# A transformer block on one Trainium2 core: where its loads are issued from, how a late modulation is spread, and a new order on every engine

## The chip, the cores and the metric

The kernel runs on one core of a Trainium2 chip. Five engines work side by side, each through its own instructions strictly in order, and wait for each other on semaphores: PE (TensorE, matmuls), DVE (VectorE), ACT (ScalarE), POOL (GpSimd) and SP (SyncE, which computes nothing and issues transfers). ACT can issue transfers too. The transfers of both queues run on the same 16 DMA engines. The metric is device time in microseconds (us) of one execution; smaller is better. Three executions of the kernel before gave 229.87, 231.78 and 234.63 us, median 231.78.

## The reference, cut to what matters

One adaptive-layernorm block over 2048 positions of width 448: a local, dilated attention and then an MLP, both scaled and shifted by six vectors that are computed from one conditioning vector `c`.

```python
mod = silu(c) @ w_mod                    # six vectors of 448: sa, ca, ga, sb, cb, gb
h = layernorm(x) * (1 + ca) + sa
q, k, v = split(h @ wqkv)                # 16 heads of 28
# each position attends to itself and 7 earlier ones, in steps of 2
o = softmax(q . k over the 8 positions) @ v
x = x + ga * (o @ wo)
h = layernorm(x) * (1 + cb) + sb
h = gelu(layernorm(h) @ w1 + b1)         # width 1792; a second layernorm, as the MLP has its own
x = x + gb * (h @ w2 + b2)
```

All inputs and the output are bf16.

## The kernel before, in words

**Layout.** The attention steps by 2, so even and odd positions never meet. A pair of neighbouring positions is kept in one partition, `s` being 0 or 1, and everything is done for both halves of 1024. `x_all` holds x in eight tiles j of 128 pairs. The contraction over 448 runs as seven blocks `kb` of 64 rows; the two halves `s` lie in partitions 0 to 63 and 64 to 127, so that two matmuls of 64 rows run beside each other. For that, wqkv, wo and w1 are loaded twice, once into each half of the partitions: 12.39 MB are read from HBM in all.

**Stages**, by the names in the plan and their lines:
- `ld`/`ldi` (431 to 475): loads. x (433), the first third of w_mod (436), wq, wk, wv (443), b1 (459), the rest of w_mod (460), wo (463), b2 as a broadcast to 128 partitions (465), w1 in four loads (470), w2 in two (474). `wpad` (453 to 457) copies wq and wk into the padded `wqk`.
- `fill` (522): eight idle matmuls at the start. `silu` (526 to 534): Exp on ACT, three small DVE operations. `mcol` (544): sa and ca as columns, on PE.
- `ln1` (559 to 578): statistics on DVE, the power -1/2 on POOL (566), normalization on DVE (578) or ACT (575, with a small DVE operation 572 before it). Tiles 0 and 1 are transposed on PE (603) and modulated on the way out (611, 613); tiles 2 to 7 are transposed by DMA, issued by SP (618, `dti`), and modulated in place (626, `hmod`).
- `qk` (648) and its evictions (657, 659), in three chunks of 256, 256 and 512 positions; `v` (681), nine windows n of 114 positions; attention per window: `lt` (716), exp on ACT (724), mask on DVE (732), `po` (745), the reciprocal and product (753, 758), `otr` (768) and its eviction (776, 778), which overwrites `hT`.
- `later_mod` (871 to 895): the other four vectors (`mbc`, 879): 16 matmuls whose stationary operand is silu(c) repeated over 128 columns, so that each vector arrives in all 128 partitions of PSUM, followed by four evictions (881 to 884); then wo is multiplied by ga (886) and w2 by gb (889), and b1 is turned into a column on PE (893).
- `wo` (792), the first residual add `x1` (795), `ln2` (two layernorms, 808 and 810 between them), its transposition by DMA (820), `w1` (840) with gelu on ACT (848), in four chunks of two tiles; `w2` (864), the second residual add `fin` (866) and the store `st` (868), per tile.

**What sets the order.** `build_plan` lists some 650 operations with their buffers, dependences and an estimated duration per engine. `Plan.solve` (299 to 396) is a list scheduler over these: at each step it takes, among what is ready on an engine, the operation of the highest priority, which is the longest way to the end plus a tuned weight per kind and tile (`CFG['weight']`, lines 35 to 239). Some operations may go to DVE or ACT (`engs` with two entries); the scheduler chooses, and it chooses the PSUM slot (four, `ps`) and the other buffers. In it a load issued on ACT is on a pretended engine of its own ("AQ"):

```python
def load(q, nbytes, fn, wr, rd=(), kind="ld"):
    a = op(kind + "i", {q: 0.07}, fn, wr=wr, rd=rd, lat=0.0)
```

so that the scheduler counts an issue as 0.07 us and not as part of ACT's row; on the chip ACT issues it, in order with its computations. A transfer also holds one of eight semaphores; the ninth transfer waits until the first has landed, on the engine that issues it, and so on in turn. In the built program SP issues x in four loads (tiles 2 and 3, then 4 to 7, then 0, then 1) and one half of wq, wk and wv. ACT issues the first third of w_mod, c, the other halves of wq, wk and wv, the rest of w_mod, wo, w1, b1, b2, fourteen in all, and behind these its first computation, the Exp of `silu`. The two w2 loads come later in its queue.

Of the kernel before, what the change touches and what calls it, by code (L numbers as in the profile page):

```python
# [28 lines left out]
 'lat': 0.12,  # L29
 'mlp_chunks': [(0, 2), (2, 2), (4, 2), (6, 2)],  # L30
 'nact': ['a01', 'a10', 'a20', 'a21', 'a41', 'a51', 'b00', 'b21', 'b30', 'b41', 'b50', 'b51', 'c01', 'c10', 'c40', 'c41', 'c61', 'c71'],
 'qk_chunks': [(0, 256), (256, 256), (512, 512)],
 'slots': 4,
 'sw': 0.13,
 'table': 1.28,
 'weight': {'b1t': -55.2,
            'cst': 151.7,
            'dti': 72.9,
            'dti:0': 58.3,
            'dti:1': 10.7,  # L40
            'dti:2': -78.3,
            'dti:3': 175.3,
            'dti:4': 75.4,
            'dti:5': 9.1,
            'dti:6': -6.2,
            'dti:7': 175.1,
            'exp': 109.0,
            'exp:0': -226.0,
            'exp:1': -49.3,
            'exp:2': -10.4,  # L50
            'exp:3': 63.6,
            'exp:4': 80.5,
            'exp:5': -70.4,
            'exp:6': 55.1,
            'exp:7': -120.8,
            'exp:8': 18.9,
            'fill': 149.6,
            'fin': -81.7,
            'gelu': 221.2,
            'gelu:0': 165.7,  # L60
            'gelu:1': -39.9,
            'gelu:2': -224.4,
            'gelu:3': 17.8,
            'hmod': 60.0,
            'hmod:1': 16.1,
            'hmod:3': 29.8,
            'hmod:7': 60.9,
            'ld': 175.5,
            'ldi': -4.4,
            'ln1': 34.3,  # L70
            'ln1:0': -94.3,
            'ln1:1': 7.0,
            'ln1:2': -47.3,
            'ln1:3': -121.9,
            'ln1:4': 56.0,
            'ln1:5': -37.3,
            'ln1:6': 36.3,
            'ln1:7': -33.1,
            'ln2': 220.1,
            'ln2:0': -94.4,  # L80
            'ln2:1': 116.0,
            'ln2:2': 217.9,
            'ln2:3': 151.4,
            'ln2:4': -199.4,
            'ln2:5': -48.9,
            'ln2:6': -25.7,
            'ln2:7': -122.3,
            'lt': 199.2,
            'lt:0': 68.1,
            'lt:1': -16.3,  # L90
            'lt:2': 5.9,
            'lt:3': 79.3,
            'lt:4': 8.4,
            'lt:5': 24.4,
            'lt:6': -33.4,
            'lt:7': 12.9,
            'lt:8': 33.1,
            'mask': -11.6,
            'mask:0': 48.2,
            'mask:1': -77.4,  # L100
            'mask:2': -20.9,
            'mask:3': 128.2,
            'mask:4': 0.8,
            'mask:5': 168.2,
            'mask:6': 40.4,
            'mask:7': -57.6,
            'mask:8': -115.1,
            'mbc': 167.8,
            'mbc:0': 46.8,
            'mcev': -12.0,  # L110
            'mcol': 135.3,
            'mod': -99.4,
            'mod:0': 147.1,
            'ms': -326.5,
            'oev': -33.6,
            'oev:0': 29.7,
            'oev:1': -27.1,
            'oev:2': -167.7,
            'oev:3': 180.5,
            'oev:4': 8.4,  # L120
            'oev:5': 244.2,
            'oev:6': -60.9,
            'oev:7': -101.9,
            'oev:8': -19.7,
            'onm': -210.0,
            'onm:0': 73.9,
            'onm:1': 22.6,
            'onm:2': -8.8,
            'onm:3': -28.6,
            'onm:4': 10.5,  # L130
            'onm:5': -105.9,
            'onm:6': 31.7,
            'onm:7': 50.6,
            'onm:8': -128.7,
            'otr': 98.6,
            'otr:0': 39.4,
            'otr:1': -2.5,
            'otr:2': -19.6,
            'otr:3': -63.1,
            'otr:4': 71.1,  # L140
            'otr:5': 165.6,
            'otr:6': 32.9,
            'otr:7': 71.4,
            'otr:8': 75.9,
            'po': 235.0,
            'po:0': -81.4,
            'po:1': -3.4,
            'po:2': 307.6,
            'po:3': 204.0,
            'po:4': -244.7,  # L150
            'po:5': 84.2,
            'po:6': 199.1,
            'po:7': -7.9,
            'po:8': 86.3,
            'qk': 10.4,
            'qk:0': -65.0,
            'qk:1': -137.4,
            'qk:2': 63.2,
            'qkev': 72.7,
            'qkev:0': 7.0,  # L160
            'qkev:1': -20.3,
            'qkev:2': 49.5,
            'rec': 317.5,
            'rec:0': 55.8,
            'rec:1': 28.4,
            'rec:2': 21.3,
            'rec:3': 152.2,
            'rec:4': -392.7,
            'rec:5': -2.8,
            'rec:6': -157.1,  # L170
            'rec:7': 32.2,
            'rec:8': 61.7,
            'silu': 202.1,
            'st': -149.8,
            'v': 63.9,
            'v:0': -96.5,
            'v:1': 98.8,
            'v:2': 119.6,
            'v:3': 24.6,
            'v:4': 63.4,  # L180
            'v:5': 87.6,
            'v:6': 31.6,
            'v:7': -39.0,
            'v:8': -8.0,
            'vev': -107.0,
            'vev:0': -80.0,
            'vev:1': 0.2,
            'vev:2': 20.3,
            'vev:3': 45.8,
            'vev:4': -107.7,  # L190
            'vev:5': -1.6,
            'vev:6': 2.8,
            'vev:7': -46.5,
            'vev:8': -111.5,
            'w1': 116.4,
            'w1:0': -16.1,
            'w1:1': 34.1,
            'w1:2': -283.9,
            'w1:3': -9.5,
            'w2': 115.9,  # L200
            'w2:0': -46.3,
            'w2:1': 137.8,
            'w2:2': 21.7,
            'w2:3': -34.0,
            'w2:4': -14.0,
            'w2:5': 22.1,
            'w2:6': -207.4,
            'w2:7': -15.4,
            'w2s': -224.4,
            'w2s:0': -33.3,  # L210
            'wo': 301.0,
            'wo:1': -26.4,
            'wo:2': 117.9,
            'wo:3': 243.1,
            'wo:4': 30.3,
            'wo:5': 79.1,
            'wo:6': 98.3,
            'wo:7': -112.6,
            'wo:8': 73.5,
            'wpad': -48.4,  # L220
            'x1': -19.1,
            'x1:1': 50.8,
            'x1:2': -11.4,
            'x1:3': 96.8,
            'x1:4': 36.8,
            'x1:5': -253.1,
            'x1:6': 98.8,
            'x1:7': -19.5,
            'x1:8': -19.3,
            'x1p': 241.6,  # L230
            'x1p:0': 66.0,
            'x1p:1': -215.7,
            'x1p:2': 39.9,
            'x1p:3': -41.0,
            'x1p:4': 2.2,
            'x1p:5': 94.5,
            'x1p:6': 151.0,
            'x1p:7': 100.6,
            'ztr': 250.0},
 'window': {'ACT': 30.25, 'AQ': 0.0, 'DVE': 0, 'PE': 0.25, 'POOL': 23.3, 'SP': 0.0}}  # L240
# [7 lines left out]
class Op:  # L248
    __slots__ = ("i", "kind", "engs", "fn", "deps", "nd", "succ", "uses", "mode", "func", "pri", "start", "end", "eng", "lat", "bump", "idx")


class Plan:
# [14 lines left out]
    def op(self, kind, engs, fn, rd=(), wr=(), uses=(), mode=None, func=ANYF, after=(), lat=None, bump=0.0):  # L267
        o = Op()
        o.i, o.kind, o.engs, o.fn, o.mode, o.func = len(self.ops), kind, engs, fn, mode, func
        o.lat = self.cfg["lat"] if lat is None else lat  # L270
# [18 lines left out]
    def _touch(self, o, key, write):  # L289
        name, lo, hi = key if isinstance(key, tuple) else (key, 0, 1)  # L290
        h = self.hist.setdefault(name, [])
# [7 lines left out]
    def solve(self):  # L299
        cfg = self.cfg  # L300
        ops = self.ops
        for o in ops:
            o.nd = len(o.deps)
            for d in o.deps:
                ops[d].succ.append(o)
        wt = cfg["weight"]
        topo, left = [o for o in ops if not o.nd], [o.nd for o in ops]
        for o in topo:
            for x in o.succ:
                left[x.i] -= 1  # L310
                if not left[x.i]:
                    topo.append(x)
# [12 lines left out]
        while ready:  # L325
            best = None
            cand = {}
            for o in ready:
                t0 = est0[o.i]
                need = {}  # L330
                for b in o.uses:
                    if b.slot is None:
                        need[b.pool] = need.get(b.pool, 0) + 1
# [723 lines left out]
```

## Time and profile before

| what | value |
|---|---|
| time, median of three | 231.78 us |
| the profiled execution's own time | 232.59 us |
| its span, from first to last instruction | 230.9 us |
| mean granted PE clock | 0.873 |
| busy: PE, DVE, ACT, POOL | 170.8, 119.7, 107.6, 42.8 us |
| read from HBM, written | 12.39 MB, 1.84 MB |
| first v matmul, first wo, first w1, last matmul's end | 48.7, 93.4, 120.2, 226.7 us |

The page cuts the span into 40 slices and gives a row per engine, each digit the busy share of a slice in tenths. PEclk is the clock that PE was granted, in tenths of full speed. DMA is the busy share of the 16 DMA engines. A timeline line reads: start, length, engine (ACTq and SPq are the queues that issue transfers), source line, operation, tiles, count, and in brackets the idle time before it and what ended it. The profiled execution's time is 1.7 us more than its span.

### The profile page before, as it was taken

The page shows a single profiled execution, that of the slowest core. Times are in us where ns is not written, and L with a number is a line of the kernel's source. Part 1 is how long each engine was busy: PE and PEld are TensorE (multiplying, and loading weights), DVE is VectorE, ACT ScalarE, POOL GpSimd, SP SyncE. Part 2 cuts the span into 40 slices and gives each one's busy share as a digit, 9 for nine tenths or more (in the row PEclk, how much of TensorE's full clock was granted, in tenths as well). Part 3 has the DMA queues.
Part 4 walks back from the last instruction along what each step waited for, and adds up shares of the span by engine and source line. Part 5 has one row for each costly group of instructions (what it writes and reads, how often), then busy time and mean ns, then how long its engine had stood idle before and what let it go on. Part 6 is the DMA issues. An engine that isn't in the chain of part 4 may idle for free. (4 is left out here: it accounts for less than half of the span.)

```text
span 230.9 us, 7200 instructions
## 1 busy us (share of the span) xinstructions
PE 170.8 (74%) x3263; PEld 116.5 (50%) x3263; DVE 119.7 (52%) x278; ACT 107.6 (47%) x145; POOL 42.8 (19%) x57
## 2 busy tenths in 40 slices
PE   5000005259958588899969998999999798999992
PEld 1000005135736366444647965896554596587551
DVE  0000009636968468779875648812998958200031
ACT  0000024414784147456764994789461487087000
POOL 6000004020511200135200305010244052110030
PEclk9755555559999659999997999999999999999999
DMA  6999999961323620000430053000021210410012
GB/s 189 310 234 281 216 206 210 203 161 34 50 43 45 179 44 3 6 0 3 26 59 4 0 43 81 7 3 3 34 44 47 43 41 3 82 42 3 0 40 80
DMA packets 23882, 17.89 MB, mean 77 GB/s; under 512 B 13612, under 2 KB 23404, under 8 KB 23852
## 3 DMA queue, kind: packets, MB, share of 16 engines
q10 hardware_dynamic: 7228, 9.35, 18.3%
q1 hardware_dynamic: 16624, 8.09, 16.8%
q8 instruction: 25, 0.41, 0.8%
q14 instruction: 5, 0.04, 0.1%
HBM read 12.39 MB, written 1.84 MB: 62 GB/s over the span
## 5 line engine op out<-in xcount | busy, mean ns | idle before, releaser
L840 PE MATMUL ps<-yT,w 64*128 64x256 bf16 x784 | 44.6, 271 | 3.8 <-DMA yT<-zb 3.3
L840 PEld LDWEIGHTS <-w 64*128 64x128 bf16 x784 | 41.7, 95 | 6.9 <-issue 5.5
L848 ACT ACTIVATE hmw<-ps,b1c 128x512 bf16<-128x512 f32 x56 | 38.2, 687 | 14.9 <-PE ps L840 8.3
L864 PE MATMUL ps<-w,hmw 128*128 128x448 bf16 x224 | 44.1, 353 | 0.8 <-ACT hmw L848 0.8
L566 POOL TENSOR_TENSOR rs<-tv,neg_half 128x2 f32<-128x2 f32 x24 | 19.2, 802 | 76.2 <-DVE tv L564 76.2
L864 PEld LDWEIGHTS <-hmw 128*128 128x128 bf16 x224 | 21.2, 98 | 20.5 <-issue 1.5
L648 PE MATMUL ps<-hT,wqk 64*128 64x256 bf16 (+1 forms) x336 | 28.6, 329 | 2.8 <-ACT vb L690 2.8
L855 POOL TENSOR_TENSOR x1p<-x_all,gbb 128x896 f32<-128x896 bf16 x8 | 16.0, 2006 | 72.6 <-DVE x_all L866 38.7
L544 PE MATMUL ps<-silu,hmw 112*64 112x1 bf16 x112 | 3.1, 192 | 30.8 <-DVE silu L532 30.8
L648 PEld LDWEIGHTS <-wqk 64*128 64x128 bf16 x336 | 17.8, 102 | 12.5 <-issue 4.2
L866 DVE TENSOR_TENSOR x_all<-ps,x1p 128x896 bf16<-128x896 f32 x8 | 8.7, 1087 | 27.1 <-PE ps L864 25.1
L559 DVE BATCH_NORM_STATS2 st<-x_all 128x6 f32<-128x448 bf16 x32 | 19.3, 603 | 0.1
L544 PEld LDWEIGHTS <-hmw 112*64 112x64 bf16 x112 | 3.2, 156 | 31.4 <-issue 26.2
L530 DVE TENSOR_SCALAR e_c<-e_c 112x4 f32<-112x4 f32 x1 | 0.2, 170 | 33.4 <-ACT e_c L526 33.4
L681 PE MATMUL ps<-wv,hT 64*64 64x448 bf16 x252 | 15.7, 392 | 1.8 <-issue 1.4
L526 ACT ACT_TABLE_LOAD x1 | 1.3, 1283 | 33.0 <-DMA wo<-in_A_wo_dram 33.0
L724 ACT ACTIVATE et<-ps 128x912 bf16<-128x912 f32 x18 | 15.7, 932 | 0.9 <-PE ps L716 0.8
L732 DVE TENSOR_TENSOR et<-et,mask 128x912 bf16<-128x912 bf16 x18 | 11.4, 654 | 8.9 <-ACT et L724 8.9
L657 ACT CAST qT<-ps 128x512 bf16<-128x512 f32 (+1 forms) x12 | 8.7, 728 | 12.2 <-PE ps L648 12.2
L792 PE MATMUL ps<-wo,hT 64*128 64x448 bf16 x112 | 13.2, 376 | 1.4 <-issue 0.9
L681 PEld LDWEIGHTS <-hT 64*64 64x64 bf16 x252 | 8.4, 119 | 7.1 <-issue 4.7
L575 ACT ACTIVATE zb<-x_all,nm,rs 128x448 bf16<-128x448 bf16 x6 | 4.5, 759 | 15.3 <-DVE nm L572 9.8
(78 smaller groups left out, 190.9 us busy)
## 6 DMA issues: line engine op xcount, KB each, us to landing
w<-in_B_w_dram ACTq DMA_DIRECT2D x6, 784.0 KB, 19.9
out_dram<-x_all SPq DMA_DIRECT2D x8, 224.0 KB, 2.1
hmw<-in_w_mod_dram ACTq DMA_DIRECT2D x1, 1568.0 KB, 14.5
x_all<-in_A_x_dram SPq DMA_DIRECT2D x1, 896.0 KB, 9.5
hmw<-in_w_mod_dram ACTq DMA_DIRECT2D x1, 784.0 KB, 8.0
w<-in_A_wqkv_dram ACTq DMA_DIRECT2D x2, 392.0 KB, 10.9
w<-in_A_wqkv_dram SPq DMA_DIRECT2D x2, 392.0 KB, 13.2
wo<-in_A_wo_dram ACTq DMA_DIRECT2D x2, 392.0 KB, 16.0
```

Of the source, the lines that this page charges most:

```text
L559: g.nc.vector.bn_stats(out=g.stats[nm][:, j, s, :], in_=src(g, pairs[j], s))
L566: op(kind, {"POOL": 0.6}, lambda g: g.nc.gpsimd.tensor_tensor(out=g.rs[nm][:], in0=g.tv[nm][:], in1=g.neg_half[:, 0:n], op=ALU.pow), rd=[" ...
L648: g.nc.tensor.matmul(o[:, s, 0:n], lhsT=g.wqk[r0:r0 + 64, kb, m, :], rhs=g.hT[r0:r0 + 64, kb, c0(t0):c0(t0 + n)], start=(kb == 0), stop=(k ...
L657: g.nc.scalar.copy(out=dst, in_=g.ps[pq.slot][:, :, 0:n])
L681: g.nc.tensor.matmul(o[64 * half:64 * half + 64, s, 0:D], lhsT=g.hT[r0:r0 + 64, kb, ka:ka + 64], rhs=g.wv[r0:r0 + 64, kb, :], start=(kb == ...
L724: g.nc.scalar.activation(out=g.ebufs[et.slot][:, 912 * hf:912 * hf + 912].rearrange("p (r c) -> p r c", r=2), in_=g.ps[lt.slot][:, :, 0:8 ...
L732: g.nc.vector.tensor_tensor(out=v, in0=v, in1=g.mask[:].rearrange("p a b -> p (a b)"), op=ALU.mult)
L792: g.nc.tensor.matmul(o[:, s, 0:D], lhsT=g.hT[r0:r0 + 64, kb, c0(128 * j):c0(128 * j + 128)], rhs=g.wo[r0:r0 + 64, kb, :], start=(kb == 0), ...
L840: g.nc.tensor.matmul(o[:, s, 0:n], lhsT=g.w1[r0:r0 + 64, kb, ft * 128:(ft + 1) * 128], rhs=g.yTb[yT.slot][r0:r0 + 64, kb, 0:n], start=(kb ...
L848: g.nc.scalar.activation(out=g.hmv(hm.slot)[:, ft, :, 0:n], in_=g.ps[p1.slot][:, :, 0:n], func=ACTF.Gelu_apprx_tanh, bias=g.b1c[:, ft:ft + 1])
L855: op("x1p", {"POOL": 2.1}, lambda g, j=j, xp=xp: g.nc.gpsimd.tensor_tensor(out=g.x1pb[xp.slot][:], in0=g.x_all[:, j], in1=g.gbb2[:].unsque ...
L864: g.nc.tensor.matmul(o[:, s, 0:D], lhsT=g.hmv(hm.slot)[:, ft, s, cc:cc + 128], rhs=g.w2[:, ft, :], start=(ft == 0), stop=(ft == FT - 1))
```

## The change

1. **Loads.** All loads go to SP, except c, the second halves of wq and wk and the first third of w_mod, which stay on ACT. They are cut smaller: x into tiles 0, 1, 2-3, 4-5 and 6-7, the rest of w_mod into two, w1 into eight pieces of 448 columns, w2 into four. In the built program SP issues: x1, x0, wq, wk (one half each), x2-3, x4-5, wv, wo, wo, wv, b2, the transposes of tiles 3 and 2, x6-7, b1, w_mod's last third, w1, w_mod's middle third, w1, the transposes of 7, 4 and 6, w1, w1, the transpose of 5, w1, the broadcasts of g2, sb and gb, w1, that of ga, w1, w2, w1, w2, w2, w2, and then the transposes of the MLP's input and the stores. ACT issues c, wq, wk, then loads its table and computes Exp, and issues the first third of w_mod behind that.
2. **Later modulation.** The four vectors are computed as four column tiles of 32, beside each other, into one row each (partitions 0, 32, 64, 96). One ACT operation evicts the rows, with a bias that adds 1 to g2's. Four DMAs on SP spread each row over 128 partitions. The first window of `wo` on PE comes after ga has been spread and multiplied into wo on DVE, as before.
3. **Order.** `Plan.solve` and its weights are gone. `Plan.place` reads a fixed order of all operations with their engines and buffers, written out in ORDER and SLOTS; the estimated durations in the plan are others. In the built order, PE runs v0, v1, qk of the first chunk, b1's transposition between, qk of the second chunk with lt, po and v2, v3 between, the modulation rows, and only then wo of tile 0; v4 to v7, po2 to po4 and qk of the third chunk follow, and then the first w1; v8 and the last step of attention 4 come after that.
4. **Small.** Sixteen idle matmuls instead of eight; an Exp on a dummy value ahead of all else on ACT; of the eight `wpad` copies, four are on POOL, three on ACT and one on DVE, where three were on ACT and five on DVE; the small operation before a normalization on ACT is done for both halves at once, and for all tiles; the last tile's add and store are done in two halves.

```diff
-    def load(q, nbytes, fn, wr, rd=(), kind="ld"):
-        a = op(kind + "i", {q: 0.07}, fn, wr=wr, rd=rd, lat=0.0)
...
+    def load(q, nbytes, fn, wr, rd=(), bulk=False):
...
+        a = op("ldi", {q: 0.6}, fn, wr=wr, rd=rd, lat=0.0, after=after, bump=0.0 if bulk else pri)
...
+    load("ACT", 900, lambda g: g.nc.scalar.dma_start(out=g.c_col[:], in_=g.c.rearrange("o (p kt) -> p (o kt)", kt=KM)), ["c_col"])
+    load_m("ACT", 0, 2, "wmA")
     load_x(0, 1)
...
+    for pc in range(4):
         for hf in range(2):
             def f(g, pc=pc, hf=hf):
+                a, b = pc * 448, pc * 448 + 448
+                g.nc.sync.dma_start(out=g.w1[64 * hf:64 * hf + 64, :, a:b], in_=g.B_w1[:, a:b].rearrange("(kb p) n -> p kb n", p=64))
+            load("SP", 401e3, f, [("w1", 2 * pc + hf, 2 * pc + hf + 1)], bulk=True)
...
     def later_mod():
-        mb = [P.buf("ps", "mb0"), P.buf("ps", "mb1")]
...
+        mb = P.buf("ps", "mrow")
+        def f_mm(g):
+            for kt in range(KM):
+                for i in range(4):
+                    g.nc.tensor.matmul(g.ps[mb.slot][32 * i:32 * i + 32, 0, 0:D], lhsT=g.silu_bc[:, kt, :], rhs=g.wmod[:, kt, (2 + i) * D:(3 + i) * D],
+                                       start=(kt == 0), stop=(kt == KM - 1), tile_position=(0, 32 * i))
+        op("mod", {"ACT": 0.65}, lambda g: g.nc.scalar.activation(out=g.mrow[:], in_=g.ps[mb.slot][:, 0, 0:D], func=ACTF.Identity, bias=g.one2[:, 0:1]),
+        for i, (nm, dst) in enumerate((("ga", "ga"), ("sb", "sb"), ("g2", "g2"), ("gb", "gb"))):
+            op("mbc", {"SP": 0.6}, lambda g, i=i, dst=dst: g.nc.sync.dma_start(out=getattr(g, dst)[:], in_=g.mrow[32 * i:32 * i + 1, :].unsqueeze(1).to_broadcast([1, 128, D])),
...
-    order = P.solve()
+    order = list(P.place(ORDER.split(), list(map(int, SLOTS.split()))))
```

More of the change, by code (lines that the diff above doesn't have):

```diff
@@ L375, in solve @@
-            o.eng, o.start, o.end = e, t, t + dur
-            free[e] = o.end
-            if e == "PE":
-                mode = o.mode
-            if e == "ACT" and o.func:
-                table = o.func
-            ready.remove(o)
-            order.append(o)
-            for b in o.uses:
-                b.left -= 1
-                if b.left == 0:
-                    last = max([o.end + cfg["lat"]] + [getattr(b, "busy", 0.0)])
-                    slots[b.pool].append((last, b.slot))
-                else:
-                    b.busy = max(getattr(b, "busy", 0.0), o.end + cfg["lat"])
@@ L753, in f_rc @@
             g.nc.vector.reciprocal(out=g.rden[rd_.slot][:], in_=o[:, :, :, DH])
-        b = op("rec", {"DVE": 0.42}, f_rc, uses=[po, rd_], after=[a])
+        b = op("rec", {"DVE": 0.35}, f_rc, uses=[po, rd_], after=[a])
         def f_on(g):
```

577 lines of the change are left out of this document (172 added, 405 removed), and 3 rows, old and new, of the table SLOTS.

## The prediction

> **What bounds the kernel now.** I read the page's slices first, then the timeline of the first 50 us, then stage windows, then the chain that ended last.
>
> ```profile
> PE   5000005259958588899969998999999798999992
> DVE  0000009636968468779875648812998958200031
> PEclk9755555559999659999997999999999999999999
> DMA  6999999961323620000430053000021210410012
> ```
>
> Slices are 5.8 us. For eight of them (to 48 us) the transfers are full and PE nearly idle; DVE wakes in the seventh. Why so late, the timeline tells:
>
> ```profile
> 16.38 13.18 ACTq L470 DMA_DIRECT2D w<-in_B_w_dram  x4
> 29.60 2.50 ACTq L459 DMA_DIRECT2D b1r<-in_B_b_dram  x1
> 32.13 0.86 ACTq L465 DMA_DIRECT2D b_bc<-in_B_b_dram  x1
> 33.03 1.28 ACT L526 ACT_TABLE_LOAD   x1 [33.03 <-DMA wo<-in_A_wo_dram]
> 34.32 0.20 ACT L526 ACTIVATE e_c<-c_col 112x4 f32<-112x4 bf16 x1
> 34.56 0.17 DVE L530 TENSOR_SCALAR e_c<-e_c 112x4 f32<-112x4 f32 x1 [33.36 <-ACT e_c L526]
> ```
>
> ACT issues 14 loads ahead of its first computation. Each reuses the semaphore of the load eight earlier and waits for it, so four w1 loads hold ACT for 13.18 us. DVE's first operation after two memsets needs ACT's Exp, so all layernorms stand behind it (33.36 us idle). PE then waits once more, for the tiny b1r load, behind w1 in the queue: useful PE work starts at 48.67 us. The stages:
>
> ```profile
> 48.50:93.40 44.90, 36.62 (x979) 26.02 (x980) 31.46 (x74) 23.95 (x36) 7.59 (x7) 0.84 0.28 61
> 93.40:120.20 26.80, 23.50 (x457) 12.01 (x450) 22.32 (x49) 15.93 (x18) 7.66 (x6) 1.00 0.17 20
> 120.20:226.75 106.55, 102.68 (x1702) 72.81 (x1702) 55.27 (x122) 60.91 (x83) 20.93 (x18) 0.98 0.14 30
> ```
>
> Columns: stretch, length, busy us of PE, PEld, DVE, ACT, POOL, PE's granted clock, DMA share, GB/s. 93.4 is the first output projection (wo), 120.2 the first w1 matmul. The last stage has 3.9 us of PE idle: little is left there. The chain that ended last agrees, with PE lines 840 and 864 at its head. So the case is the head, to wo.
>
> **Part 1: when PE starts.** Afterwards ACT issues four loads only, Exp stands before the last, and DVE begins with x. The binding load becomes wv: the first PE group is v, and SP issues wv's second half after wo's halves. Ahead of it or with it: six x tiles 1.38 MB, wq, wk, wv, wo 3.21 MB, the first w_mod third 0.80 MB. Rates by windows of before: 307 GB/s over 4 to 12 us (x and w_mod, 112 or 128 partitions), 204 over 12 to 16 and 185 over 26 to 32 (64-partition loads of 896-byte rows). 3.21/0.204 + 2.18/0.307 = 22.8 us, plus 2.1 before data flow and 1 to land: v at **26 us**, 22.7 sooner. mcol, transposes and modulation of the first 256 positions fit before (at 35.2 to 45.1, ten us, in before; from w_mod's landing near 13 they end by 23).
>
> The w1 loads become half as large. [...]
>
> **Part 2: from v to wo on PE.** In row durations: v 4 x 1.52, qk 16 x 0.79 (4.76 for six), lt 8 x 0.37, po 2 x 0.64, otr 2 x 0.41. The modulation: four groups took 3.39 us one after another; as four column tiles between a quarter of it and all of it, I take 0.87, by v's rate (28 matmuls of four tiles, 1.52). Sum 24.8 us. PE starts cold: the clock was 0.50 until 52.6, 4 us after work began, costing 2 us. Before, the stage left 8.3 us idle; bounds 0 and 8.3, I take 5. PE could do wo at 26 + 24.8 + 2 + 5 = **57.8**.
>
> **Part 3: when wo may start.** wo must first be scaled by ga, now a DMA from a row in SBUF to 128 partitions, on SP, after the row's eviction by ACT and six of eight w1 pieces. Behind SP's wait for that row stand the rest of w1 and w2 and all yT transposes; behind DVE's wait for ga stand the masks of attention 2 and 3, the last modulation tile and the first layernorm 2. Ahead of ga: 64-partition loads 5.62 MB, between 27.5 us (204) and 30.4 (185), I take 29; others 4.36 MB/0.307 = 14.2; six hT transposes at 1.4 (two filled 2.8 us of the transfers at 56 to 60) = 8.4; four broadcasts, never seen: 112 KB at the 344 GB/s of 48 to 49 us, where b2's broadcast landed, is 0.33 each, a transpose's rate makes 1.4, and b2's whole way from issue to landing, 16.6, is the far end. I take 0.6 each, nearest b2's bytes. 2.1 + 29 + 14.2 + 8.4 + 2.5 + 2 to land = **58**; scaling (1.79, line 886) makes wo 60, two us behind PE. So both chains meet near 60; before, wo stood at 93.4. Transfers now share these 58 us with PE work that before came after them.
>
> **Part 4: from wo to w1.** PE: wo 3 x 1.5, po 3 x 0.64, v 4 x 1.52, qk2 8 x 1.54 (7.72 for five), otr 2 x 0.41, lt 2 x 0.37 = 26.4, to 86. DVE from 58: scale of wo 1.79, of w2 2 x 1.75, four masks at 0.65, two x1 at 1.09, two onm with rec at 1.3, eight statistics pairs at 0.78, four h passes at 0.64, small ones 2.2: 23.5; two POOL round trips 1.5, the transpose 2.9 from issue: 86. I take 87, that is 27 after wo; before it was 26.8. w2 lands 1.6 MB after ga, 8 us: about when DVE asks.
>
> **Part 5: the rest.** w1 to the last matmul: 106.55, plus v8 (1.52) and otr4 (0.4), which now come later: 108.5, to 195.5. The new order can gain at most the 3.9 idle, or lose as much at ACT, whose in-order queue has layernorm pieces between gelus; I take nothing. Tail: 226.75 to 230.9 was 4.15; the last add and store in halves save half of 1.09 and 0.2: 3.5, span 199.
>
> Costed at nothing: the doubled fill (8 x 0.36, before mcol; uncovered 3 us); the early table load (1.28, while loads land); four weight copies on POOL (nearest row, its 128x912 copy, 1.03; they end before qk, else 1 us each); one eviction instead of four (ACT 1.1, not on the path); the merged nm operations; b1r, now behind the last x (near 31 us, PE at it 32).
>
> **The sum.** The profiled execution took 232.59 us, its span 230.9. 199 + 1.7 = 200.7; that execution stood 0.8 above the median of 231.78, so **200 us**, own range 193 to 208 (ga 55 to 63 by the bounds on rates and broadcasts, last stage plus or minus 3.9).
>
> **Rivals.**
> - Fast loads (0.15): everything flows at 307 GB/s, as two queues' halves together might. ga lands at 2.1 + 32.5 + 8.4 + 1.3 + 2 = 46, v starts at 21, PE reaches wo at 48, twelve sooner: **188**. Against: 26 to 46 us held 185 to 205.
> - Cold PE (0.22): PE is fed in drips, and its clock stays low from v to wo. For: 75 to 90 us of before, with PE 60 to 80% busy after gaps of 1.4 and 2.8 us, got 0.68, 0.50, 0.80. At their mean 0.66, 24.8 becomes 37.6, wo comes at 69, and the end is **209**; at 0.50, 221. Against: DVE has all x early, so fewer gaps. [...]
> - SP takes ACT's place (0.08): SP stops at transposes 3, 7, 5 and at the modulation rows for data that its own later loads delay, and the queue runs dry. At 6 us for each of the four, 24 later: **224**. Then the move does not do what it says. For: SP's waits before a transpose reached 28.9 us. Against: up to eight loads, some 3 MB or 14 us, stand in front.
> - Slower (0.05): the four broadcasts run one by one out of single partitions, and DVE and PE stand at wo meanwhile. From 9.9 us each, 37 in all, the time passes 237; at b2's 16.6 it is **264**. Against: b2's way was mostly queue.
>
> **Chances.** Forecast 0.50, the others as above. A measurement tells from no change about 2%, 227 to 236. Faster 0.91, same 0.04 (the upper part of the SP case), slower 0.05. The range 186 to 220 holds the forecast, the fast case but its lower tail and most of the cold one.
>
> **What would show it.** Right: first v near 26, ga landing near 58, wo near 60, w1 near 87, then about 108 us. Wrong: DVE waiting for ga well past 60 (broadcast or SP), a clock below 0.8 between 30 and 60 (cold), holes in the DMA row before 55 (SP), or more than 6 us of PE idle after the first w1 (the new order).

## The result, and the profile after

The changed kernel took 208.50 us (median of four, 204.44 to 211.99), the kernel before 232.88 beside it (229.87 to 234.63): a ratio of 0.889, 95% interval 0.868 to 0.911. The ratio is taken over the faster executions, 204.44 and 206.00 against 229.87 and 231.78; the changed kernel's other two took 211.00 and 211.99. The profiled execution took 204.44 us, its span 202.4, at a mean granted clock of 0.916 (0.873 before). The forecast was 200, its range 186 to 220.

| us, profiled executions | before | forecast | after |
|---|---|---|---|
| first v matmul | 48.7 | 26 | 26.19 |
| PE could do wo | – | 57.8 | 64.08 |
| ga landed | – | 58 | 65.06 |
| first wo | 93.4 | 60 | 66.91 |
| first w1 | 120.2 | 87 | 95.90 |
| last matmul's end | 226.7 | 195.5 | 199.0 |
| execution | 232.59 | 200.7 | 204.44 |

The page's slices of after, 5.06 us each: PE, DVE, the granted clock, the transfers' busy share and what they moved.

```profile
PE   7206289759476698999999999999979999999993
DVE  3407759735542787997836875598675797100213
PEclk9855569996957699999999999999999999999999
DMA  6999989999989940007002004000221003210101
GB/s 159 247 269 229 208 215 225 197 170 163 138 117 117 237 150 3 0 3 94 3 3 50 3 11 133 3 0 3 49 49 49 0 3 91 45 50 3 45 23 70
```

DVE works from the first slice and PE from the sixth (before: seventh and ninth). But PE has holes from the eighth to the fourteenth slice (35 to 71 us), the clock falls to 0.5 to 0.7 in four of them, and from the ninth on the transfers are still 80% busy or more while the bytes fall to 117 GB/s. The forecast had none of the three. By stage (columns as in the prediction):

```profile
26.20:66.90 40.70, 30.07 (x793) 21.68 (x793) 21.95 (x56) 21.75 (x31) 7.00 (x9) 0.84 1.06 174
66.90:95.90 29.00, 27.12 (x578) 13.60 (x579) 23.95 (x50) 17.81 (x22) 8.73 (x6) 0.95 0.38 75
95.90:199.00 103.10, 101.62 (x1762) 70.07 (x1758) 58.45 (x129) 62.19 (x84) 21.04 (x18) 1.00 0.12 30
```

The first stage lost: 10.6 us idle and 30.07 busy, where 7 (5 and the wait for ga) and 26.8 were reckoned. The last gained: 1.5 us of idle at full clock, where before had 3.9 at 0.98. From the first w1 on, ten of the eleven kernels profiled with this order of PE took between 108.2 and 109.2 us to the end of the execution, so the case is decided ahead of w1. Where the first stage stopped, PE's timeline of after tells:

```profile
38.25 0.28 PE L484 MATMUL ps<-qT,kT 28*64 28x57 bf16 x11
39.55 0.62 PE L484 MATMUL ps<-qT,kT 28*64 28x57 bf16 x53 [1.03 <-issue]
...
42.28 0.93 PE L416 MATMUL ps<-hT,wqk 64*128 64x256 bf16 x13
45.48 1.44 PE L416 MATMUL ps<-hT,wqk 64*128 64x256 bf16 x15 [2.27 <-issue]
...
49.72 0.61 PE L513 MATMUL ps<-vb,et 64*64 64x29 bf16 x53
51.67 0.27 PE L513 MATMUL ps<-vb,et 64*64 64x29 bf16 x11 [1.34 <-issue]
...
53.65 0.39 PE L536 MATMUL ps<-ident,on 57*64 57x57 bf16 x25
57.05 0.26 PE L536 MATMUL ps<-ident,on 57*64 57x57 bf16 x3 [3.01 <-issue]
...
66.91 2.79 PE L560 MATMUL ps<-wo,hT 64*128 64x448 bf16 x14 [2.83 <-DVE wo L664]
```

PE stops in the middle of a run of like matmuls, after 11 of 64, 13 of 28, 53 of 64, 25 of 28, and waits for nothing that the profile shows ("issue"). Count the matmuls between two stops: 53 lt, 14 qk, 16 of the modulation, 32 lt and 13 qk make 128; 15 qk, 32 lt, 28 v, 53 po: 128; 11, 28, 64, 25: 128. (The next two, seen in runs below: 3, 42 qk, 28, 55 lt; and 73 lt, 14 wo, 41 po.) With a weight load each (the page counts 3271 of either) that is 256 instructions. The profile has a queue named "instruction", 25 packets of 16 KB over the execution, one for each 256 or so of PE's 6542 instructions; one begins at 36.7, 43.1, 48.8 and 54.6, each ahead of the end of one of the four stops. So I read the stops as PE waiting for its own program; a table behind the experiments shows how closely the two go together. The kernel before has such stops too, without a stream: 1.40 us at 67.7, with the transfers at 1 GB/s, and 0.86 at 94.1, 640 matmuls further on.

I call these places A (38.5), B (43.2), C (50.3), D (54.0), E (inside the next lt, 73 matmuls from its end), F (po, 41 of 64) and G (otr, two from its end, near 91). PE's order is the same in every kernel below that starts from the changed one, so the places stay at the same instructions.

### The profile page after: what moved, and what is told of

It is laid out like the page before. It is cut to its first block, busy times and chain, and to the rows that moved or that the text cites. A ratio compares the mean times of both kernels' runs of the same rounds, so it can differ in the third digit from the quotient of the medians.

```text
span 202.4 us, 7245 instructions
## 1 busy us (share of the span) xinstructions
PE 168.7 (83%) x3271; PEld 111.9 (55%) x3271; DVE 117.3 (58%) x275; ACT 109.5 (54%) x149; POOL 44.5 (22%) x63
## 3 DMA queue, kind: packets, MB, share of 16 engines
q10 hardware_dynamic: 1520, 1.61, 3.4%
## 4 chain that ended last, share of the span: by engine, by line
PE 65%; DMA 20%; ACT 4%; SPq 4%; issue 3%; DVE 2%; ACTq 1%
PE ps L610 21%; PE ps L634 17%; PE ps L416 11%; DMA wv<-in_A_wqkv_dram 8%; PE ps L560 6%; PE ps L449 6%; DMA w<-in_A_wqkv_dram 4%; DMA ga<-mrow 4%; DMA yT<-zb 4%; SPq L221 2%; SPq L661 2%; PE ps L513 2%; ACT et L492 2%; PE ps L484 1%; ACT zb L343 1%
## 5 line engine op out<-in xcount | busy, mean ns | idle before, releaser
L618 ACT ACTIVATE hmw<-ps,b1c 128x512 bf16<-128x512 f32 x56 | 37.7, 687 | 13.6 <-PE ps L610 10.6
L610 PEld LDWEIGHTS <-w 64*128 64x128 bf16 x784 | 38.5, 94 | 5.9 <-issue 0.7
L330 POOL TENSOR_TENSOR rs<-tv,neg_half 128x2 f32<-128x2 f32 x24 | 20.4, 851 | 78.0 <-DVE tv L328 77.6
L625 POOL TENSOR_TENSOR x1p<-x_all,gbb 128x896 f32<-128x896 bf16 x8 | 15.2, 1894 | 44.8 <-issue 29.9
L416 PEld LDWEIGHTS <-wqk 64*128 64x128 bf16 x336 | 17.1, 101 | 11.6 <-issue 2.9
L643 DVE TENSOR_TENSOR x_all<-ps,x1p 128x896 bf16<-128x896 f32 x7 | 7.6, 1090 | 20.3 <-PE ps L634 20.2
L458 ACT CAST vb<-ps 128x896 bf16<-128x896 f32 x8 | 7.2, 910 | 15.2 <-PE ps L449 15.2
L343 ACT ACTIVATE zb<-x_all,nm,rs 128x448 bf16<-128x448 bf16 x9 | 6.3, 753 | 14.0 <-DVE nm L333 14.0
L563 DVE TENSOR_TENSOR x_all<-ps,x_all 128x896 bf16<-128x896 f32 x8 | 8.7, 1084 | 8.4 <-PE ps L560 8.4
L343 ACT ACTIVATE zb<-h,nm,rs 128x448 bf16<-128x448 bf16 x12 | 8.7, 753 | 7.6 <-DVE nm L333 5.1
L526 DVE TENSOR_TENSOR on<-ps,rden 128x896 bf16<-128x896 f32 x9 | 9.8, 1085 | 2.9 <-PE ps L536 2.7
```

What stands on the lines that cost most here:

```text
L330: op(kind, {"POOL": 0.8}, lambda g: g.nc.gpsimd.tensor_tensor(out=g.rs[nm][:], in0=g.tv[nm][:], in1=g.neg_half[:, 0:n], op=ALU.pow), rd=[" ...
L343: g.nc.scalar.activation(out=dst(g), in_=src(g), func=ACTF.Identity, scale=g.rs[nm][:, idx:idx + 1], bias=g.nm[nm][:, idx:idx + 1])
L416: g.nc.tensor.matmul(o[:, s, 0:n], lhsT=g.wqk[r0:r0 + 64, kb, m, :], rhs=g.hT[r0:r0 + 64, kb, c0(t0):c0(t0 + n)], start=(kb == 0), stop=(k ...
L610: g.nc.tensor.matmul(o[:, s, 0:n], lhsT=g.w1[r0:r0 + 64, kb, ft * 128:(ft + 1) * 128], rhs=g.yTb[yT.slot][r0:r0 + 64, kb, 0:n], start=(kb ...
L618: g.nc.scalar.activation(out=g.hmv(hm.slot)[:, ft, :, 0:n], in_=g.ps[p1.slot][:, :, 0:n], func=ACTF.Gelu_apprx_tanh, bias=g.b1c[:, ft:ft + 1])
L625: op("x1p", {"POOL": 2.05}, lambda g, j=j, xp=xp: g.nc.gpsimd.tensor_tensor(out=g.x1pb[xp.slot][:], in0=g.x_all[:, j], in1=g.gbb2[:].unsqu ...
```

## The experiments

**First and second: the queue alone.** Kernel before, with ten of ACT's loads and both w2 loads issued by SP; then also b1's small load first.

```diff
-g.nc.scalar.dma_start(out=g.b1r[:], ...        # likewise wv, w_mod's rest, wo, b2, w1, w2
+g.nc.sync.dma_start(out=g.b1r[:], ...
```
```diff
     order = P.solve()
+    b1 = next(o for o in order if o.i == 30)
+    order.remove(b1)
+    order.insert(1, b1)
```

> The kernel before, its scheduler untouched, with ten of the loads that ACT issued ahead of Exp (half of wv, the rest of w_mod, wo, w1, b1, b2) and the two w2 loads issued by SP at the same places of the order. Theory A, the whole head was ACT's queue: Exp runs near 4 us instead of 34, layernorm starts when x lands near 12, v starts near 26 and the end comes about 20 us sooner, 212. Theory B, there were two locks on the head: PE stands at b1's transposition, whose load is still behind w1 in the queue and lands near 47, so v starts near 47, only 2 us sooner; but the layernorms of tiles 2 to 7 are done by then and the first modulated second chunk is ready sooner (70.5 in before, near 62 now): about 225.

> As the run before it, and b1's load moved to the second place of the order. Theory A: no further gain, 212 in both. Theory B: this takes the second lock away, v starts near 24, but SP now issues all loads before the first transposition of the second chunk, which lands behind w1 near 48; the second chunk of qk starts near 50 instead of 70.5 and the end comes about 18 us sooner than before: 214. Left over to the changed kernel would then be its order and its spread rows, some 6 us.

Measured: 229.04 us, ratio 0.989 (0.983 to 0.995), and 218.23 us, 0.948 (0.940 to 0.957). PE's timeline of the first:

```profile
18.88 1.67 PE L603 MATMUL ps<-ident,zb 128*128 128x128 bf16 x14 [4.42 <-ACT zb L575]
50.69 0.19 PE L893 MATMUL ps<-ident,b1r 14*128 14x14 bf16 x1 [30.14 <-DMA b1r<-in_B_b_dram]
```

and of the second:

```profile
30.12 5.44 PE L681 MATMUL ps<-wv,hT 64*64 64x448 bf16 x56 [9.14 <-DMA wv<-in_A_wqkv_dram]
...
55.21 1.36 PE L716 MATMUL ps<-qT,kT 28*64 28x57 bf16 x96 [10.00 <-ACT kT L657]
```

With the issuing queue alone DVE's first layernorm starts at 12.62 and not at 35.05, and PE's transposes at 18.88 and not at 40.13. But PE then waits 30 us for 3.5 KB of b1 (6.75 in the kernel before), and v begins at 50.81, 2 us later than before: two locks in a row, and opening one gives 1%, less than either theory asked. With both open, 5% (214 us was asked); then wv sets v's start, at 30.12, and PE's ten us pass while ACT and DVE wait (8.86 and 9.51 us) for the transposes of h, which SP issues from 37.55 on, behind w1 and the first of w2. The other half of the gain belongs to the rest of the change: the order of loads and of work, the spread rows and the small edits. No run here takes these apart.

**Third: ga first.** The changed kernel with the spread of ga ahead of the others.

```diff
 # ORDER, SP's words (188 ga, 190 g2, 189 sb, 191 gb; 38 to 52 w1; 63 to 69 w2)
-40S 46S 146S 44S 190S 189S 191S 50S 188S 48S
+40S 46S 146S 188S 44S 190S 189S 191S 50S 48S
```

> The changed kernel with one line of the order moved: ga is spread first, before g2, sb, gb and one w1 piece. If ga's landing (65.1) alone holds wo, ga lands near 56 and wo starts near 58, 8 us sooner, and the end comes 6 to 8 us sooner. If PE reaches wo at 64.1 by its own chain, as the trace shows it, wo starts at 64 to 65 and the gain is 2 to 3 us at most.

Measured: 210.11 us, 0.909 (0.904 to 0.914); profiled 209.15. The time is no better than the changed kernel's. ga landed at 56.3, nine us sooner, and wo began at 66.71, no sooner than in after (66.91), waiting for attention's exponentials and not for ga. The stops had grown: 0.74, 2.00, 1.61, 4.65 at A to D, 3.88 at F. The wait for ga was no lock of its own; PE was as late by its stops.

**Fourth: bulk loads late.** The spreads as in the third, and all w2 and w1 loads behind them.

```diff
-26S 34S 28S 38S 24S 42S 162S 138S 154S 40S 46S 146S 44S 190S 189S 191S 50S 188S 48S 63S 52S 65S 67S 69S
+26S 34S 28S 24S 162S 138S 154S 146S 188S 190S 189S 191S 63S 65S 67S 69S 38S 40S 42S 44S 46S 48S 50S 52S
```

> The changed kernel with all w1 and w2 loads issued behind the spread rows, ga first; the PE order is the same. Theory F: the PE gaps inside runs of matmuls that wait for nothing (1.0 at 38.5, 2.3 at 43.2, 1.3 at 50.3, 3.0 at 54.0) are the fetch of PE's next instructions, slowed by the loads; with the loads gone from 27 to 50 us each of the four falls to 1.4 or less (the 1.4 of before, where the transfers were quiet), the clock stays up, transposes land in 3 to 4 us instead of 5 to 6, and wo starts near 57: the end 6 to 9 us sooner, unless w2 or w1 then lands too late (w2 near 58, w1 near 76, asked for at 75 and 96 in the changed kernel). Theory G: the gaps are waits on other engines; they keep their lengths, and wo gains only what an earlier ga gives, 2 to 3 us.

Measured: 199.65 us, 0.856 (0.848 to 0.863), its interval below that of the changed kernel (0.868 to 0.911). A, B and C were gone and D had 1.12. wo began at 61.39, 5.5 us sooner than in after (57 was asked): 1.9 of it comes from shorter stops, 2.5 from the wait for ga and 2.1 from qk behind D at full clock, and a wait of 1.2 for a mask takes from that. But E and F opened:

```profile
54.67 0.62 PE L490 MATMUL ps<-qT,kT 28*64 28x57 bf16 x55 [0.33 <-ACT kT L431]
59.96 1.07 PE L490 MATMUL ps<-qT,kT 28*64 28x57 bf16 x73 [4.66 <-issue]
```

The loads were issued from 54.97 on, and F (64.9 to 66.15) stands under them, at 308 GB/s. E doesn't. While it lasted, the transfers were 80% busy and moved little:

```profile
55.30:59.90 4.60, 0.00 (x0) 0.00 (x0) 0.91 (x1) 0.05 (x1) 0.00 (x0) 0.90 0.80 57
```

That is the mark of the four spreads, as the runs without w1 show below; the last was issued at 50.98 and landed 10.2 us later. So a stop goes with whatever the transfers do at it and just ahead of it, loads or spreads.

**Fifth: wv's second half ahead of wo**, on top of the fourth.

```diff
-20S 30S 32S 18S
+20S 18S 30S 32S
```

> The kernel of the fourth experiment (all w2 and w1 loads behind the four spread rows, ga first; 199.65 us) with one issue moved more: wv's second half goes out ahead of wo's two halves instead of behind them. In the fourth experiment PE waits 4.45 us for it, until v at 26.3. Theory H (the head's last loads set everything up to wo): v starts near 22, when the transposed tiles are ready, and wo, the first w1 matmul and the end all come 4 us earlier: wo at 57.5, time 195.5. Rival (other chains, tiles 2 to 7 and the modulation rows, gate what follows v): v starts at 22 but second-chunk qk stays near 51.4 and wo near 61, time 199 to 200.

Measured: 199.06 us (195.95 to 206.06), 0.859 (0.848 to 0.871): no difference from the fourth that the runs show. In the profiled execution, 195.95 and the shortest of all kernels, v began at 24.47, held by ACT's last piece of hT and no more by wv, wo at 58.48, w1 at 87.72; E still had 4.39. The move is worth two us at v; the spread between executions is wider.

**Two bulk loads in flight**, on top of the fourth: each late load overlaps the one two places before it.

```diff
-                a, b = pc * 448, pc * 448 + 448
+                a, b = pc * 448 - (8 if pc else 0), pc * 448 + 448
...
-    for (a, b) in ((0, 4), (4, 7), (7, 11), (11, 14)):
+    for (a, b) in ((0, 4), (7, 11), (3, 7), (10, 14)):
```

> The kernel of the fourth experiment (199.65 us), but each of the twelve late w2 and w1 loads reads a strip that the load two places earlier wrote (the same values), so that it waits for that one to land: two bulk loads in flight instead of up to eight, 0.3 MB more bytes in all. In the fourth experiment PE has a gap of 4.66 us at 55.2 within a run of lt matmuls that waits for nothing, with a packet of PE's instructions inside it and eight loads queued. Theory Q (PE's instruction fetch waits behind the bytes that the loads have queued): the gap shrinks below 2 us, wo comes near 58, time 197. Rival S (any full stream of transfers slows the fetch, however deep the queue): a gap of 4 to 5 us stays and the time with it, 199 to 200. The loads take until 84 at worst, ahead of w1 at 92, so they cost nothing else.

Measured: 203.11 us, 0.883 (0.874 to 0.892). E fell to 2.04, as the theory of the queue's depth asks, but F had 1.54 and G, which the loads reach now (177 GB/s over 76 to 90), 1.27; and PE stood 3.02 us for a mask at 46.5, before any late load was issued (1.21 in the fourth). E stands under the spreads here too (43 GB/s over 51 to 58), which the edit leaves alone, and PE came to it 2.3 us later than in the fourth. So the run settles nothing on the depth, and it is slower.

**What the spreads do.** Two variants of the changed kernel: the spreads from 128 partitions instead of one; and w1 left out but for one seventh (so not the reference's MLP).

```diff
-in_=g.mrow[32 * i:32 * i + 1, :].unsqueeze(1).to_broadcast([1, 128, D])
+in_=g.b2_bc[:]
```
```diff
-g.nc.sync.dma_start(out=g.w1[64 * hf:64 * hf + 64, :, a:b], in_=g.B_w1[:, a:b].rearrange("(kb p) n -> p kb n", p=64))
+g.nc.sync.dma_start(out=g.w1[64 * hf:64 * hf + 64, 0, a:b], in_=g.B_w1[0:64, a:b])
```

> The changed kernel, with the four spreading transfers reading the 128x448 tile of b2 (128 partitions) instead of one row in one partition each; bytes, order and waits stay, and the later modulation's values are left out of the result. In the changed kernel they took 6.7 to 8.5 us from issue to landing, and ga came at 65.06, 8.3 after its issue at 56.8. Theory R (a single partition as the source of 128 descriptors is what makes them slow and holds the transfers at 107 to 133 GB/s): they land in 3 to 4 us, ga near 61, wo by PE's 64, time 3 us less, near 205.5 by the slower or 201.5 by the faster of the changed kernel's runs. Rival (they stand in the queue behind the w1 loads like everything else): 6 to 8 us again, wo at 66 to 67, no gain.

> The changed kernel, with six sevenths of every w1 load left out (each of the eight issues fetches 64 rows of 896 bytes; the rest of w1 is zeros from one memset on DVE while it waits for x), so the MLP's result is not the reference's; PE's program is the same. Theory F (PE's gaps inside runs of matmuls, 1.03 us at 38.5, 2.27 at 43.2, 1.34 at 50.3, 3.01 at 54.0, 0.83 at 70.2, are its instruction fetch held up by the bulk loads): those up to 57 shrink to 0.5 us or nothing, the granted clock over 46 to 62 is above 0.85, PE is ready for wo by 57, ga lands near 56, the time is 198 to 200; the gap at 70 stays with the w2 loads. Rival (the fetch, or the program's own order, makes these gaps whatever the loads): gaps of 1 to 3 us at the same instructions, wo not before 62.

Measured, one execution each: 204.89 and 202.86 us. The times say little beside the changed kernel's 204.44 to 211.99; the traces say more. With the wide source two spreads landed in 5.3 and 4.6 us (6.7 to 8.5 in after), the transfers moved 257 GB/s over 56 to 66 (122 in after), and DVE scaled wo at 64.69 without waiting for ga; but D grew to 5.09 and the end stayed. Without w1, A, B and C shrank to 0.61, 0.63 and 0.42, as theory F said; D, against it, grew to 4.65. The transfers of that run from 49 to 53 us:

```profile
DMA  9199922599550995228995509952299949599742
GB/s 54 9 36 54 36 9 9 18 54 36 18 18 0 54 54 18 9 9 27 45 36 18 18 0 54 54 18 9 9 45 45 81 72 236 36 54 72 63 36 45
DMA packets 168, 0.16 MB, mean 39 GB/s; under 512 B 11, under 2 KB 167, under 8 KB 167
## 3 DMA queue, kind: packets, MB, share of 16 engines
q1 hardware_dynamic: 167, 0.14, 81.3%
q8 instruction: 1, 0.02, 1.4%
```

The engines are 81% busy at 39 GB/s: 0.813 x 16 x 4 us over 167 packets is 0.31 us for each, where the late loads of the fourth experiment took 0.065 (108.7% of 16 engines over 9 us, 2426 packets). The copies that all read one SBUF partition held the engines here without moving much, and a packet of the instruction queue lies among them (52.36 to 53.24).

**Both gone.** The last two edits together.

> The run without w1's loads (one seventh of each is left, the rest of w1 is zeros), and also the four spreading transfers reading a 128x448 tile from 128 partitions instead of one row in one partition each, so the later modulation's values are left out too. In the run without w1's loads the early gaps within PE's matmuls shrank (1.03 to 0.61, 2.27 to 0.63, 1.34 to 0.42 us), but one of 4.65 us stood at 50.2, three instructions before the end of an otr group, while the spreads alone kept the transfers 81% busy at 39 GB/s. Theory G (a spread from one partition occupies the DMA engines and holds up PE's instruction fetch just as bulk loads do): with both gone the gap is below 1 us, the transfers are nearly idle over 50 to 56, the spreads land in 2 to 3 us, PE is ready for wo by 57 to 58, and the time is 197 to 199. Rival (the gap belongs to PE's own stream of short instructions): 3 to 5 us at the same otr group, time 201 to 203.

Measured, one execution: 196.53 us.

```profile
53.38 0.22 PE L537 MATMUL ps<-ident,on 57*64 57x57 bf16 x3 [1.45 <-issue]
...
62.76 0.37 PE L514 MATMUL ps<-vb,et 64*64 64x29 bf16 x23 [1.22 <-issue]
```

These are D and F, the only stops left before w1 of more than 0.3 us; I had asked for less than 1 at D. D: 4.65 with the spreads from one partition, 1.45 without, all else alike. The clock was 1.00 from 36 to 90 us, wo began at 58.62 and w1 at 88.02, 7.9 us sooner than in after. So the stops go with both kinds of transfer: with the bulk loads at A, B and C, and at D with either alone (4.65 with the spreads, 5.09 with the loads and a wide source).

**Issued by ACT.** The changed kernel with wo, b1, b2, w1 and w2 issued by ACT at the same places of the order.

```diff
-g.nc.sync.dma_start(out=g.w1[...                # likewise wo, b1, b2, w2
+g.nc.scalar.dma_start(out=g.w1[...
```

> The changed kernel, with wo, b1, b2, w1 and w2 (sixteen loads) issued by ACT, each at the same place of the written order, instead of SP; everything else stays. Theory B (the issuing queue matters because a reused semaphore holds the issuing engine): ACT, whose evictions and layernorm pieces stand between those loads, waits for a load eight transfers back several times, 2 to 8 us each, PE's matmuls wait for ACT's evictions, first v is past 28, wo past 72, the time 212 to 225. Rival (only the order of the loads matters): v at 26 to 27, wo at 66 to 68, time 204 to 210.

Measured, one execution: 207.64 us, within what the rival gave; wo began at 70.60, between the two theories. v began at 25.43 and ACT was not held up by loads; one late transposition kept DVE idle for 8.07 us, PE then 6.99 for a mask. A to D don't stop in this run: ACT reaches its w1 loads at other times, the transfers moved 96 GB/s over 34 to 42 us (183 in after), and C's packet came while PE waited for the mask. With this order the issuing engine matters little for the time. What held ACT in the kernel before was fourteen loads placed ahead of its first computation.

**Two tries for a better kernel.** On top of the fifth, the rows go to HBM and are spread from there; and then also all w2 and w1 loads behind the first residual sum.

```diff
+                if i == 0:
+                    g.nc.sync.dma_start(out=g.rows[:], in_=g.mrow[0:128:32, :])
+                g.nc.sync.dma_start(out=getattr(g, dst)[:], in_=g.rows[i:i + 1, :].to_broadcast([128, D]))
...
+    g.rows = drp.tile([4, D], BF16, name="rows")        # drp: a pool in DRAM
```
```diff
+            if a == 0:
+                g.nc.sync.dma_start(out=g.gate[:], in_=g.x_all[0:1, 0, 0, 0:64])
# ORDER: the twelve loads moved behind 271D, the first residual sum
```

> The kernel of the fifth experiment (bulk loads behind the spreads, wv's second half ahead of wo; 199.06 us, its faster runs 195.95 to 199.39), with the four rows written once to HBM (3.5 KB) and spread by four loads from there, instead of from one SBUF partition each. There ga landed 6.4 us after its issue at 44.77, and a gap of 4.39 us stood at 52.7 in PE's lt matmuls, spreads and w2's first loads flowing. Theory G (the spreads at 38 to 45 GB/s hold up the fetch): the write takes 2 us, the four spreads land within 3 to 4 us more (112 KB each at 300 GB/s is 0.4), ga at 50, gap below 1.5 us, wo 3 us earlier, median 196. Rival S (any stream holds up the fetch, and w2's loads now flow through the same place): the gap stays at 4 to 5 us, time 199.

> The kernel of the run with the rows in HBM (200.44 us; wo at 60.2), with a store of 128 bytes of the first residual sum ahead of the twelve w2 and w1 loads in SP's queue, and these moved behind that sum in the order, so that no load starts before about 64 us. There, gaps of 1.80 us at 57 (lt) and 4.66 us at 63.4 (po) stood in PE while w2 and w1 ran at 258 GB/s. Theory F (bulk transfers hold up the fetch): with no transfer but transposes and spreads before 64 the first gap falls below 1 us and the second below 1.5, wo comes at 58 to 59, the clock stays at 1.00 from 50 to 66, and w1 at 90; the loads (4.8 MB at 205 to 230 GB/s) end at 87, before w1 needs them, and PE's matmuls of that stretch are long ones (v, qk of 512), which use few instructions per us: median 194 to 196. Rival 1 (the gaps only move to where the loads go): gaps of 3 to 5 us in all over 66 to 88, median 199 to 201. Rival 2 (w2 or w1 land too late): DVE waits for w2 at 72, PE for w1 past 90, median over 201.

Measured: 200.44 us, 0.870 (0.865 to 0.875), and 201.25 us, 0.870 (0.863 to 0.877); profiled 204.18 and 203.11. From HBM the last three spreads landed in 3.5 to 4.4 us (6.4 to 10.1 in the fifth), and over 50 to 51.5 us, where they flow alone, a packet took 0.053 us (23.6% of 16 engines, 106 packets) and not 0.31. But w2 and w1 then began 51.7 us into the run, and the stops were E 1.80 and F 4.66. With the gate:

```profile
56.00:66.00 10.00, 8.21 (x304) 5.58 (x298) 8.62 (x14) 6.75 (x9) 2.24 (x2) 1.00 0.04 10
66.00:76.00 10.00, 8.64 (x106) 4.13 (x104) 7.43 (x16) 6.26 (x8) 4.14 (x4) 1.00 1.05 261
76.00:90.00 14.00, 8.93 (x254) 5.24 (x252) 8.23 (x21) 8.12 (x11) 1.87 (x3) 0.98 1.19 187
```

Over 56 to 66 the transfers are idle, and neither E nor F stops; wo began at 60.13. Over 76 to 90, with 187 GB/s, G stops, and w1 began at 94.74:

```profile
83.92 0.38 PE L546 MATMUL ps<-ident,on 57*64 57x57 bf16 x26
89.07 0.21 PE L546 MATMUL ps<-ident,on 57*64 57x57 bf16 x2 [4.77 <-issue]
```

That is the first rival of its expectation: the gap only moves. I had taken the stretch for one of long matmuls, and it has two windows of v and one of attention in it. The stops in us, by run and place (a dash: none over 0.3; the fifth has 0.62 and the run with two in flight 0.49 at two further multiples of 128):

| run | A | B | C | D | E | F | G |
|---|---|---|---|---|---|---|---|
| after | 1.03 | 2.27 | 1.34 | 3.01 | – | 0.83 | – |
| ga first | 0.74 | 2.00 | 1.61 | 4.65 | – | 3.88 | – |
| bulk late (fourth) | – | – | – | 1.12 | 4.66 | 1.27 | – |
| wv first (fifth) | – | – | – | 1.23 | 4.39 | 0.40 | – |
| two in flight | – | – | – | – | 2.04 | 1.54 | 1.27 |
| wide source | 1.18 | 1.45 | 1.36 | 5.09 | 1.14 | – | – |
| bulk on ACT | – | – | – | – | 1.24 | – | – |
| no w1 | 0.61 | 0.63 | 0.42 | 4.65 | – | 0.83 | – |
| no w1, wide source | – | – | – | 1.45 | – | 1.22 | – |
| rows in HBM | – | – | – | – | 1.80 | 4.66 | – |
| loads after the sum | – | – | – | – | – | – | 4.77 |

Where the time of a stop passes, the packets of 16 KB tell. In the table: when PE began the first matmul behind the multiple of 128 before, when the packet for the next 256 instructions began and ended in the transfers, and when PE went on behind the multiple that it belongs to.

| run, place | multiple before | packet | PE goes on | stop |
|---|---|---|---|---|
| no w1, wide source, D | 49.56 | 50.42 to 51.73 | 53.38 | 1.45 |
| no w1, D | 47.81 | 52.36 to 53.24 | 54.83 | 4.65 |
| loads after the sum, E | 54.43 | 56.36 to 57.29 | 58.77 | – |
| bulk late (fourth), E | 51.29 | 57.50 to 58.42 | 59.96 | 4.66 |
| no w1, wide source, G | 79.65 | 80.70 to 82.00 | 83.32 | – |
| loads after the sum, G | 80.65 | 86.32 to 87.70 | 89.07 | 4.77 |

At all 35 stops of the table before, PE went on 1.2 to 1.7 us after the end of a packet, and the packet itself took 0.9 to 1.5. What differs is its start: in the table, 0.9 to 1.9 us after the multiple before where PE stops briefly or not at all, 4.5 to 6.2 where it stops for over 4.6. So the length of a stop goes with the packet's start, and not with the packet's own time.

The best kernels are the fourth and the fifth, 3 to 4% below the changed one by their ratios to before. They don't remove the stops either: in sum 8.48 us in after, 7.05 and 6.64 in these two.

## Why the prediction was right, and where it was not

The sign, the range and the stages were right. The median, 208.50, lies 8.5 above the forecast of 200, inside 186 to 220 and just past the sum's own 193 to 208. The sum came within 3.7 us of the profiled execution, and that is in part luck, for errors cancel: 6.9 late at wo, 2 more to w1, 5.4 gained after it.

- **Part 1 (v at 26): right.** v began at 26.19, waiting 4.52 us for wv as named. The sum has no price for the halved w1 loads: before, the transfers moved 204 GB/s over 12 to 16 us, with loads of 392 KB, and 205 over 32 to 46, with loads of 784 KB. After, their slices are 80% busy or more from 5 to 71 us; no run tests the halving alone.
- **Part 2 (PE ready for wo at 57.8): failed by 6.3.** Two terms were too small: busy time, 26.8 with the 2 us of cold clock against 30.07 (the rows named add up to 24.7, not 24.8), and the 5 us of idle against 7.8 without the wait for ga. The four stops A to D make 7.65 of the 7.8. The bounds of that term, 0 and 8.3, held, but I had argued it from the kernel before, where this stage ran with the transfers at 28%; the step "transfers now share these 58 us with PE work that before came after them" was seen and given no price. The modulation as four column tiles took 0.94 us (0.87 taken, 3.39 before).
- **Part 3 (ga at 58): failed by 7.** The term that was too small is 0.6 us for a broadcast. At the 39 GB/s of the run without w1 one holds the transfers for 2.9 us (114,688 bytes), the four for near 12 and not 2.4. But the sum counted bytes, and ga came by a chain: stops A and B (3.3 us) put off the rows, which ACT evicted by 49.0; SP issued three broadcasts and a w1 load until 56.80, and ga landed 8.3 us after that. With ga issued first it landed at 56.3, broadcasts as slow as before. That both chains meet held: 64.08 and 65.06, and bringing ga sooner alone gained nothing (ga first, wide source).
- **Part 4 (27 us from wo to w1): 29.** Stop F (0.83) and 27.12 busy us for 26.4.
- **Part 5 (108.5 us after w1): 103.1.** "At most the 3.9 idle" was no bound: the granted clock rose from 0.98 to 1.00 as well, and 2.4 of the idle went. The tail was 3.4 (3.5).
- **Rivals.** The cold clock came true in part: 0.84 over the stage, 0.50 from 57 to 63. It came behind the stops B (0.60) and D (0.50), not with drips of data: PE waited there for nothing that the profile shows. SP in ACT's place did not happen as told: the transfers were nearly idle for 1.4 us only, from 49.6, though SP's issue of ga 7.8 us after the rows were evicted is of its kind. Fast loads and single-file spreads did not come, though the second was right about the single partition, at 2.9 us and not 9.9.

What is not settled: a stop lasts 0.4 us in one run and 5 in another at the same place under a like stream. The packet then starts late in the one and not in the other; why, the records don't show.

## What to carry to other kernels

Count the instructions of the engine that bounds the kernel: here the instruction queue moved 16 KB for every 256 or so of PE's 6542, stretches of short matmuls ran through 256 in 2.4 to 4.9 us (from one stop of after to the next, A to D), and with a stream of loads or slow copies under them PE stopped in the middle of a run for up to 5.09 us. When a head is emptied by issuing loads earlier, price what the loads then meet. A row landed sooner on 128 partitions from HBM (3.5 to 4.4 us, behind a write of 3.5 KB) than from one partition of SBUF (6.4 to 10.1 in the fifth).

## What the runs showed of the hardware

- PE's "issue" gaps of more than 0.3 us between A and G lie, in every profiled run of the new order, at multiples of 128 matmuls with their weight loads, and each ends 1.2 to 1.7 us after a packet of 16 KB of the instruction queue. With no w1 and a wide source A, B and C vanish and D is 1.45; with the rows spread from HBM and bulk loads held back until 65 us all up to F vanish.
- The 112 KB spreads from one SBUF partition ran at 39 GB/s with the 16 engines 81% busy, 0.31 us for a packet of 896 bytes (no w1, 49 to 53 us); in the late loads of such packets one took 0.065 (fourth experiment, 63 to 72 us).
- Behind the stops of 2.27 and 3.01 us the granted clock read 0.60 and 0.50, behind the one of 1.34 it read 1.00. Windows of after that follow the stops of 2.27, 1.34 and, twice, 3.01 us (third number from the end: the clock):

```profile
47.40:49.90 2.50, 2.50 (x60) 1.38 (x56) 1.56 (x4) 1.59 (x3) 0.00 (x0) 0.60 1.84 177
51.60:54.00 2.40, 2.33 (x128) 1.89 (x128) 1.97 (x4) 0.60 (x1) 0.00 (x0) 1.00 1.13 169
57.00:59.00 2.00, 1.95 (x21) 1.43 (x23) 1.65 (x3) 0.05 (x1) 0.00 (x0) 0.50 0.81 135
59.00:61.00 2.00, 2.00 (x22) 1.47 (x20) 0.41 (x2) 1.09 (x2) 0.93 (x1) 0.50 0.89 135
```

The stop at D thus costs twice: 42 qk matmuls behind it took 4.66 us, and 2.56 in the fourth experiment, whose clock was 1.00 there.
